# Threshold attention and a SwiGLU block: one weight join moved behind the masks, value passes ahead of transposes, two more nested groups, and a changed plan for the last part

## The chip, the cores and the metric

The kernel runs on one core of a Trainium2 chip. The metric is the time of one execution on the device in microseconds (us); lower is better. Engines are named as the profile names them: PE is TensorE (matrix products and transposes), DVE is VectorE, ACT is ScalarE, POOL is GpSimd, SP is the engine that issues the DMAs.

## The reference

```python
# q, k, v: (8 batches, 8 heads, 576, 64) fp32; tau = 0.02
scores = matmul(q, k^T) / sqrt(64)
thresh = max(scores, -1) - tau
scores = where(scores >= thresh, scores, -1e9)
scores = scores - max(scores, -1)
attn = exp(scores); attn = attn / (sum(attn, -1) + 1e-9)
x = matmul(attn, v)            # -> (4608 tokens, 512)
g = x @ w_gate                 # w_gate, w_val: (512, 1536)
out = (g * sigmoid(g) * (x @ w_val)) @ w_out   # w_out: (1536, 512)
```

Everything is fp32, results included.

## The kernel before

The heads are taken in pairs, 32 in all, four for each batch. The kernel has three parts.

**The first part (0 to about 129 us)** works through batch 0 in eight passes, `n` = 0 to 7, in an order written out by hand: passes 0 to 3 take the first two query tiles of each of the four pairs, passes 4 to 7 the remaining three, of which the last is a short tile (`t == NT`). For each tile TensorE computes scores into a PSUM bank (L484), VectorE takes the maximum (L501), ScalarE the exponential (L505), and VectorE the mask, which multiplies by "score at or above the threshold" and sums (L508). The masks are the last readers of the scores' banks, one for each head. Then the rows are scaled by the reciprocal of the sum (ScalarE L518, POOL L516), transposed on TensorE (`tp`, L552 and L554, the rest in `end`, L560), copied out by ScalarE (L561), and multiplied with the values (`attend`, L585 and L587). A generator for each tile, `go`, is advanced step by step, and the loop places other work between its steps:

- `fill(part)` issues products of the feed-forward block's first weights for tokens that are there already (`pg`, `pv`, L601), as many as `pace` gives to a tile. ScalarE reads `pg` at L616 and L617.
- The weights of the block come from HBM in pieces. A piece is fetched by two DMAs on SP (`fetch_weights`, L332), split by ScalarE into an upper and a lower word (`split_weights`, L348 and L349), clamped by POOL (L341), shifted by VectorE (L368), joined by VectorE with the sign bits (`join_weights`, L374), and its lower part is added by POOL (`add_lower`, L384). `join_weights` takes all the pieces that were shifted, which is two after a short tile: that tile calls `shift_weights(2)`. It stands right behind the maxima, ahead of the tile's exponentials and masks.

**The middle (129 to about 1127 us)** takes batches 1 to 7 in 28 passes of three tiles each, 84 slots. The order on TensorE is written out; that of VectorE, ScalarE, POOL and SP comes from a planner. `Plan` keeps a list of open jobs for each of these engines. A job has a length in us (`took`), dependencies, a rank (a lower one goes first among those that are ready within .2 us) and a delay of its result (`lag`). `pe()` puts work on TensorE, advances the plan's clock, and makes the jobs that start before it issue their instructions. The lengths are constants in the code, so the order is fixed when the kernel is built. `slot_rest` holds the jobs of one slot: maxima, exponentials (L2104), masks (L2106), the exchange of sums (`xj`, ScalarE L2115), sum and reciprocal (`rj`, VectorE L2120 and L2121), scaling (ScalarE L2133, POOL L2130), transposes on VectorE (L2135). `POOLED` says how many of a slot's scalings are POOL's.

The tokens of the feed-forward block go in nine chunks `c` of 512: chunks 0 to 7 are the first 512 rows of each batch, chunk 8 the last 64 rows of all eight. Between the slots' products the gate and value products of a chunk that is complete are placed, in six groups `g` by `gates_and_values(c)`. A `Group` computes a 2x2 block product with seven products instead of eight: blocks of weights and of tokens are added before, and results after. One product is four matmuls of 128x128 by 128x256 (L1138). In a `NestedGroup` the products p5 and p3 are split once more, each into seven matmuls of 128x128 by 128x128 (L1333); their inputs are made by `deepen_x` on VectorE, the results are copied by ScalarE (L1271, L1273) and added up by `fold`, four additions on VectorE or POOL (helpers at L929 and L926). `deep = c > DEEP and g in WITH_BLOCKS`, with `DEEP = 2` and `WITH_BLOCKS = (1, 2, 3)`, chooses between them. The class `Deep` does the output product in the same manner, with inner sums of gated values (`inner_sums`), results combined from two PSUM banks (`combine`, L2018 and L2020 on VectorE), and deepened products `px`, `py` (L1768).

**The last part (from about 1127 us)** has no attention tile left. `tail[0]` is set, the tokens of the last two chunks, 7 and 8, are deepened (`deepen_all`), twelve groups of class `Whole` follow, six for each chunk (products L2543; L2593 is ScalarE's tanh of a folded gate, L2595 multiplies it with the value on VectorE, L2615 and L2625 add a product to a sum and are the last readers of its PSUM bank), and then the output products of `Deep(7)` and `Deep(8)`, whose sums end in `out_dram`.

Of the kernel before, what the change touches and what calls it, by code (L numbers as in the profile page):

```python
# [14 lines left out]
ALU = mybir.AluOpType  # L15
# [12 lines left out]
class Plan:  # L28
# [3 lines left out]
    HOP, PIPE = 0.08, 0.22  # L32
    PATIENCE = 0.2
    AGE = 12.0

    def __init__(self):
        self.t = self.moved = 0.0
        self.free = dict.fromkeys(("DVE", "ACT", "POOL", "SP"), 0.0)
        self.open = {e: [] for e in self.free}

    def job(self, eng, took, fn, *deps, rank=1, lag=0.0, moves=0.0):
# [30 lines left out]
    def step(self):  # L72
        start, e, n = self.peek()
        j = self.open[e].pop(n)
        start = max(start, j.ready)
        j.fn()
        self.free[e] = start + j.took
        j.end = start + j.took + j.lag
        if j.moves:
            self.moved = max(self.moved, start) + j.moves  # L80
            j.end = max(start + j.took, self.moved) + j.lag
# [63 lines left out]
def kernel(  # L145
# [11 lines left out]
    nc = tc.nc  # L157
    P = 128
    B, H, S, D = q.shape
    NP = H // 2  # L160
# [209 lines left out]

    def join_weights():
        for up, place, lo in shifted:
            ub = up.bitcast(U32)
            nc.vector.scalar_tensor_tensor(out=ub, in0=words(place, up, 1), scalar=0x80000000, in1=ub,  # L374
                                           op0=ALU.bitwise_and, op1=ALU.bitwise_xor)
            used.discard(place)
        unsummed.extend(shifted)
        shifted.clear()
        add_lower(min(1, len(unsummed)))
# [407 lines left out]
    for n, seg in enumerate(segs[:2 * NP]):  # L787
        early_slots[0] = n < NP
        if n >= NP:
            seg["v"] = segs[seg["i"]]["v"]  # L790
        for x, t in enumerate(seg["tiles"]):
            assert n < NP or seg["i"] in turned_rests
            go = scores(seg, t)
            next(go)
            steps(n, x, "maxima")
            if n >= NP:
                join_weights()
            if not n and not x:
                run_idle(6)
            next(last, None)  # L800
            box = []
            if n < NP:
                attend_tile(lambda *y: box.extend(y))
            else:
                attend_tile()
            flips = flip_steps()
            if n >= NP and x == 1:
                next(flips, None)
            next(go)
            if box:  # L810
                box[1]()
                give_back(box[0])
            next(last, None)
            for _ in flips:
                pass
            if n == NP and x == 0:
                attend_tile()
                give(FIRST)
            part = pace(n, x) / 2
            more = len(split)  # L820
            if n >= NP:
                split_weights()
                fetch_weights(2)
            steps(n, x, "flipped")
            next(go)
            steps(n, x, "masked")
            double = t == NT and NP <= n < NP + 3
            if n >= NP:
                clamp_split()
                add_lower(1)  # L830
                if more and not double:
                    shift_weights()
            fill(part)
            next(go)
# [90 lines left out]
    def pool_tt(out, a, b, op):  # L925
        return lambda: nc.gpsimd.tensor_tensor(out=out, in0=a, in1=b, op=op)  # L926

    def dve_tt(out, a, b, op):
        return lambda: nc.vector.tensor_tensor(out=out, in0=a, in1=b, op=op)  # L929

# [330 lines left out]
    class Seven(Buf):  # L1261
# [13 lines left out]
        def fold(self, eng, rank, *deps):  # L1275

            y = self.place.rearrange("p (x q) -> p x q", q=P)
            tt, took, less = (dve_tt, 0.36, 0.23) if eng == "DVE" else (pool_tt, 0.85, 0.52) if tail[0] else (pool_tt, 0.75, 0.44)
            twice = lambda x: y[:, x:x + 1].broadcast_to((P, 2, P))
            j = job(eng, took, tt(y[:, 1:3], twice(0), y[:, 1:3], ALU.add), *deps, rank=rank)  # L1280
            j = job(eng, took, tt(y[:, 0:7:6], twice(2), y[:, 5:7], ALU.add), j, rank=rank)
            j = job(eng, less, tt(y[:, 2], y[:, 0], y[:, 3], ALU.add), j, rank=rank)
            return job(eng, took, tt(y[:, 4:6], twice(6), y[:, 4:6], ALU.add), j, rank=rank)

# [390 lines left out]
    class Deep:  # L1675
# [65 lines left out]
        def inner_sums(self, o, a, place, ready, *deps):  # L1741

            a11, a21, a12, a22 = quarters(a)
            flat = place if len(place.shape) == 2 else place.rearrange("p f n -> p (f n)")
            s1, s2, s3, s4 = (flat[:, n * QW:(n + 1) * QW].rearrange("p (f q) -> p f q", q=P) for n in range(4))
            tt, eng, took = (dve_tt, "DVE", 0.55) if tail[0] else (pool_tt, "POOL", 1.0)
            rank = 0 if o == 1 and self.c == B - 1 else 0 if o == 1 else 1 if o == 5 or o in (3, 6) and not tail[0] or o in (0, 6) and tail[0] or self.c == B - 2 else 2
# [45 lines left out]
        def combine(self, q, *deps, psum=False):  # L1793
# [13 lines left out]
            else:  # L1807
                tt, eng, took, less, rank = (dve_tt, "DVE", 0.36, 0.23, 1) if tail[0] else (pool_tt, "POOL", 0.75, 0.44, 2)
            twice = lambda x: x.broadcast_to((P, 2, P))
# [147 lines left out]
        def p5(self):  # L1957
# [3 lines left out]
            state["free_cells"] = lambda *deps, m=m: self.free_cells((5, 6), m, *deps)  # L1961
            n, j = self.combine(t7, job("POOL", 2.2, pool_tt(t7, t7, t, ALU.add), *self.c5, *self.c7, rank=1))
            self.ship(1, 1, n, j)
# [99 lines left out]
    def slot_rest(seg, t, pss, mark, pooled, max_by_act, rank):  # L2063
# [52 lines left out]

        xj = job("ACT", 0.78, exchange, *masks.values(), rank=1)

# [3 lines left out]

        rj = job("DVE", 0.36, total, xj, rank=1)
        sum_users[-1].append(rj)
# [101 lines left out]
    def gates_and_values(c):  # L2226
# [5 lines left out]
        for g in range(NF2):  # L2232
            deep = c > DEEP and g in WITH_BLOCKS
            new = NestedGroup(c, g) if deep else Group(c, g)
# [42 lines left out]
    CH = {0: 2, 1: 3, 10: 4, 11: 4}  # L2277
    POOLED = {0: 3, 1: 1, 2: 1, 3: 3, 4: 3, 5: 2, 6: 1, 7: 2, 8: 1}
    MAX_BY_ACT = (0, 1, 3, 4, 5, 6, 8, 9)
# [13 lines left out]
    def block_part(b, kk):  # L2293
# [17 lines left out]
        if kk in GV:  # L2311
            if kk == 1:
                state["gv"], state["c"] = gates_and_values(c), c
                if c > DEEP:
                    deepen_x(c, *(j for js in streamed_kept.values() for j in js))
# [22 lines left out]
    for s, (n, x) in enumerate((n, x) for n in range(len(halved)) for x in range(NU3)):  # L2338
# [21 lines left out]
        if s == 1:  # L2360
            prepare_v(seg)
        at_, pooled, max_by_act = (kk, POOLED, MAX_BY_ACT) if b > DEEP else (s, FIRST_POOLED, FIRST_MAX_BY_ACT)
        slot_rest(seg, t, pss, mark, pooled.get(at_, 0), at_ in max_by_act, 1 if x == NU3 - 1 else 2)
# [27 lines left out]

    tail[0] = True
    last_x = []
# [15 lines left out]
    load_last(1, 1, attended)  # L2409
    state["free_cells"](attended)  # L2410

# [20 lines left out]
    def deepen_all(c, eng, rank, lo, n, step, fourth, *deps, last=()):  # L2432
# [5 lines left out]
        t4 = deep_places[c][2][:, os_] if fourth is None else fourth  # L2438
        tt, took = (dve_tt, 0.15 + 0.18 * n) if eng == "DVE" else (pool_tt, 0.2 + 0.32 * n)
        j = job(eng, took, tt(t1, b12, b11, ALU.subtract), *deps, rank=rank)  # L2440
# [272 lines left out]
```

## Time and profile before

| what | value |
|---|---|
| time, median of 3 runs | 1345.34 us (1344.86 to 1345.55) |
| the profiled execution: its own time | 1344.29 us |
| the profiled execution: its span | 1342.4 us |
| mean granted TensorE clock | 0.999 |
| PE busy | 1327.0 us, 99% of the span |
| DVE, ACT, POOL busy | 1082.9, 899.1, 932.8 us (81%, 67%, 69%) |
| DMA moved | 209.81 MB, 156 GB/s in the mean |

All start times in this text are us from the start of the span. The profile records each fp32 matmul twice, so counts of matmul rows are twice the program's. "Busy" is time in which an engine executes; instructions that issue a DMA or wait are not counted. A row of a timeline gives the start, the length, the engine, the line, the operation, what it writes and reads, the shape, and a count where equal instructions follow each other; in square brackets stands the idle time ahead of it and what ended it. The name of a buffer in a row is that of its place in memory, which many values share in turn.

### The profile page before, as it was taken

The page shows a single profiled execution, that of the slowest core. Times are in us where ns is not written, and L with a number is a line of the kernel's source. Part 1 is how long each engine was busy: PE and PEld are TensorE (multiplying, and loading weights), DVE is VectorE, ACT ScalarE, POOL GpSimd, SP SyncE. Part 2 cuts the span into 40 slices and gives each one's busy share as a digit, 9 for nine tenths or more (in the row PEclk, how much of TensorE's full clock was granted, in tenths as well). Part 3 has the DMA queues.
Part 4 walks back from the last instruction along what each step waited for, and adds up shares of the span by engine and source line. Part 5 has one row for each costly group of instructions (what it writes and reads, how often), then busy time and mean ns, then how long its engine had stood idle before and what let it go on. Part 6 is the DMA issues. An engine that isn't in the chain of part 4 may idle for free. (4 is left out here: it accounts for less than half of the span.)

```text
span 1342.4 us, 41686 instructions
## 1 busy us (share of the span) xinstructions
PE 1327.0 (99%) x16274; PEld 1123.1 (84%) x16274; DVE 1082.9 (81%) x2891; ACT 899.1 (67%) x2341; POOL 932.8 (69%) x1115
## 2 busy tenths in 40 slices
PE   9999999999999999999999999999999999999998
PEld 7777877787887878888888888888888889999998
DVE  7888898888887778888888887888888887667886
ACT  6888777767756677787777777777777775344300
POOL 2688497565685759857895779677976799856720
PEclk9999999999999999999999999999999999999999
DMA  8852424356557553656365746655474627565241
GB/s 180 205 188 92 85 58 134 122 150 178 154 166 220 174 167 89 208 165 219 76 201 168 232 111 187 178 168 149 115 214 146 213 68 232 158 202 183 88 169 40
DMA packets 230884, 209.81 MB, mean 156 GB/s; under 512 B 167968, under 2 KB 185376, under 8 KB 223008
## 3 DMA queue, kind: packets, MB, share of 16 engines
q1 hardware_dynamic: 226768, 206.22, 52.2%
q8 instruction: 129, 2.11, 0.7%
q10 hardware_dynamic: 3920, 0.92, 0.3%
q14 instruction: 67, 0.55, 0.1%
HBM read 169.08 MB, written 38.01 MB: 154 GB/s over the span
## 5 line engine op out<-in xcount | busy, mean ns | idle before, releaser
L2106 DVE SCALAR_TENSOR_TENSOR pall<-sc,th,pall 128x288 f32<-128x288 f32 x504 | 244.2, 513 | 42.6 <-ACT pall L2104 23.4
L2104 ACT ACTIVATE pall<-sc,nm 128x288 f32<-128x288 f32 x504 | 232.9, 498 | 35.3 <-DVE pall L2106 34.9
L2135 DVE STREAM_TRANSPOSE pall<-pall 128x576 f32<-128x576 f32 x252 | 188.3, 764 | 22.1 <-ACT pall L2133 12.1
L1138 PE MATMUL pb<-xall,big 128*128 128x256 f32 x864 | 205.8, 381 | 0.0
L2133 ACT ACTIVATE pall<-pall,ri 128x288 f32<-128x288 f32 x388 | 178.9, 527 | 27.7 <-DVE ri L2121 26.9
L926 POOL TENSOR_TENSOR big<-big 128x128 f32<-128x128 f32 (+3 forms) x214 | 158.9, 751 | 46.5 <-ACT big L1273 20.8
L1138 PEld LDWEIGHTS pb<-xall,big 128*128 128x128 f32 x864 | 161.2, 190 | 24.0 <-issue 2.2
L926 POOL TENSOR_TENSOR hall<-hall,tmp 128x512 f32<-128x512 f32 x80 | 102.3, 1279 | 95.6 <-DVE hall L1197 75.9
L2079 DVE TENSOR_REDUCE mx<-sc 128x2 f32<-128x576 f32 x168 | 125.7, 748 | 39.7 <-PE sc L2058 39.3
L2058 PE MATMUL sc<-kT,qT 64*32 64x288 f32 (+1 forms) x5376 | 145.3, 345 | 0.4 <-DVE pall L2106 0.4
L1138 PE MATMUL pa<-xall,big 128*128 128x256 f32 x576 | 137.7, 382 | 0.0
L2058 PEld LDWEIGHTS sc<-kT,qT 64*32 64x32 f32 x5376 | 96.2, 106 | 48.6 <-issue 9.3
L2157 PE MATMUL xa<-pall,vall 64*32 64x288 f32 x4032 | 129.4, 404 | 0.5 <-PE px L1768 0.4
L1138 PEld LDWEIGHTS pa<-xall,big 128*128 128x128 f32 x576 | 107.8, 190 | 17.5 <-issue 2.5
L2157 PEld LDWEIGHTS xa<-pall,vall 64*32 64x32 f32 x4032 | 75.6, 107 | 46.6 <-issue 5.0
L2130 POOL TENSOR_SCALAR pall<-pall,ri 128x288 f32<-128x288 f32 x116 | 58.2, 513 | 53.1 <-DVE ri L2121 52.8
L1138 PE MATMUL pe<-xall,big 128*128 128x256 f32 x384 | 91.4, 381 | 0.0
L2115 ACT COPY sums<-sums 32x6 f32<-32x6 f32 x336 | 66.6, 198 | 30.3 <-DVE pall L2106 25.2
L1138 PEld LDWEIGHTS pe<-xall,big 128*128 128x128 f32 x384 | 72.4, 190 | 11.1 <-ACT pall L2133 0.7
L2081 DVE TENSOR_REDUCE mx<-sc 128x1 f32<-128x288 f32 x168 | 75.0, 447 | 0.0
L926 POOL TENSOR_TENSOR hall<-hall 128x384 f32<-128x384 f32 (+2 forms) x69 | 70.0, 1028 | 0.8
L1196 ACT ACTIVATE vall<-tmp 128x512 f32<-128x512 f32 x72 | 45.1, 627 | 35.6 <-POOL tmp L926 19.0
(365 smaller groups left out, 3051.6 us busy)
## 6 DMA issues: line engine op xcount, KB each, us to landing
big<-sums_hbm SPq DMA_DIRECT2D x30, 1280.0 KB, 7.9
big<-sums_hbm SPq DMA_DIRECT2D x30, 1024.0 KB, 7.8
vall<-in_v_dram SPq DMA_DIRECT2D x112, 144.0 KB, 3.5
big<-sums_hbm SPq DMA_DIRECT2D x54, 256.0 KB, 3.6
sums_hbm<-big SPq DMA_DIRECT2D x36, 256.0 KB, 3.8
out_dram<-big SPq DMA_DIRECT2D x32, 256.0 KB, 2.8
qT<-in_q_dram SPq DMA_DIRECT2D x112, 72.0 KB, 4.0
kT<-in_k_dram SPq DMA_DIRECT2D x112, 72.0 KB, 3.0
```

Source lines behind the costliest of these rows:

```text
L926: return lambda: nc.gpsimd.tensor_tensor(out=out, in0=a, in1=b, op=op)
L1138: nc.tensor.matmul(ps[:, i], w[:, k_, i * P:(i + 1) * P], x[:, k_, :], start=first and i == k_ == 0, stop=True, skip_group_check=True)
L2058: nc.tensor.matmul(pss[h][(slice(g * G, (g + 1) * G), *part)], qT[hs, col:col + G], kT[hs, c * SH + keys[0]:c * SH + keys[1]], start=True, ...
L2079: rs.append(job("DVE", 0.72, lambda n=n, tile_=tile_: nc.vector.tensor_reduce(out=mx[:, n:n + 2, 0], in_=tile_[:, :, 0:SH], axis=AX.X, op= ...
L2081: rs.append(job("DVE", 0.42, lambda n=n, tile_=tile_: nc.vector.tensor_reduce(out=mx[:, n + 2:n + 3, 0], in_=tile_[:, :, SH:SH + SQ], axis ...
L2104: ej = job("ACT", 0.42, lambda x=x, n=n: nc.scalar.activation(ps[x], scs[x], AF.Exp, bias=nm[:, n:n + 1]), ej, masks.get((h, u - 1)), rank=0)
L2106: masks[x] = job("DVE", 0.45, lambda x=x, n=n: nc.vector.scalar_tensor_tensor(out=ps[x], in0=scs[x], scalar=th[:, n:n + 1], in1=ps[x], op0 ...
L2115: nc.scalar.copy(sm[g * G:(g + 1) * G, 0:m, 1], sm[o * G:(o + 1) * G, 0:m, 0])
L2130: scaled.append(job("POOL", 0.48 if seg["i"] >= 3 * NP else 0.4, lambda x=x, n=n: nc.gpsimd.tensor_scalar(out=x, in0=x, scalar1=ri[:, n:n ...
L2133: scaled.append(job("ACT", 0.46, lambda x=x, n=n: nc.scalar.activation(x, x, AF.Copy, scale=ri[:, n:n + 1]), rj, rank=rank))
L2135: seg["turned"].append(job("DVE", 0.72, lambda both=both: nc.vector.transpose(out=both, in_=both), *scaled, rank=rank))
L2157: nc.tensor.matmul(holds[a].ap()[x * G:(x + 1) * G, 0:SH].rearrange("d (i q) -> d i q", q=G), vr[rs, h, j, ds], p[rs, h, :, j, :], start=( ...
```

## The change

It has three pieces.

1. In the first part, `join_weights` gets a count. Behind the maxima one piece is joined; what is left is joined behind the masks, and the two fetches that its place allows are issued there. In the short tile of passes 4 to 7 half of the tile's `fill` is issued ahead of the transposes, and the other half is halved again for the two places behind.
2. Groups 2 and 3 of chunk `c = 2` become nested: `deep` is `c >= DEEP` with `WITH_BLOCKS[1:]` at `c == DEEP`, and `deepen_x` is called for that chunk too.
3. For the last part the planner gets new numbers: a model in which VectorE and POOL lengthen each other where jobs with all operands in SBUF overlap (`SLOWED`, used once `plan.shares` is set together with `tail[0]`), other lengths for folds, inner sums and deepening, a delay of .3 for folds, other ranks for the inner sums, the deepening of chunk 8 and the last tile's sums, POOL for two scalings of the last tile, a later due time of the freed cells, and VectorE instead of POOL for one addition and one combination of `Deep(7)`.

```diff
@@ Plan
+    SLOWED = {"DVE": 0.45, "POOL": 0.2}
...
-        self.free[e] = start + j.took
-        j.end = start + j.took + j.lag
+        took = j.took
+        if self.shares and e in self.SLOWED and getattr(j.fn, "in_sbuf", False):
+            for x, (k, end) in self.last.items():
+                if x != e and end > start:
+                    both = min(end - start, took)
+                    took += both * self.SLOWED[e]
+                    k.end += both * self.SLOWED[x]
+                    self.free[x] = max(self.free[x], k.end - k.lag)
+                    for i in k.then:
+                        i.ready = max(i.ready, self.after(k, i.eng))
+            self.last[e] = j, start + took
+        self.free[e] = start + took
+        j.end = start + took + j.lag
@@ first part
-    def join_weights():
-        for up, place, lo in shifted:
+    def join_weights(n=None):
+        steps = shifted[:n]
+        for up, place, lo in steps:
...
-        unsummed.extend(shifted)
-        shifted.clear()
+        unsummed.extend(steps)
+        del shifted[:n]
         add_lower(min(1, len(unsummed)))
...
             if n >= NP:
-                join_weights()
+                join_weights(1)
...
+            first_fill = n >= NP and t == NT
+            if first_fill:
+                part = pace(n, x) / 2
+                fill(part)
             next(go)
...
-            part = pace(n, x) / 2
+            part = part / 2 if first_fill else pace(n, x) / 2
...
             if n >= NP:
+                if shifted:
+                    join_weights()
+                    fetch_weights(2)
                 clamp_split()
@@ NestedGroup.fold
-... else (pool_tt, 0.85, 0.52) if tail[0] else (pool_tt, 0.75, 0.44)
+... else (pool_tt, 0.73, 0.46) if tail[0] else (pool_tt, 0.75, 0.44)
...
-            return job(eng, took, tt(y[:, 4:6], twice(6), y[:, 4:6], ALU.add), j, rank=rank)
+            return job(eng, took, tt(y[:, 4:6], twice(6), y[:, 4:6], ALU.add), j, rank=rank, lag=0.3 if tail[0] else 0.0)
@@ Deep.inner_sums
-            tt, eng, took = (dve_tt, "DVE", 0.55) if tail[0] else (pool_tt, "POOL", 1.0)
-            rank = 0 if o == 1 and self.c == B - 1 else 0 if o == 1 else 1 if o == 5 or ...
+            tt, eng, took = (dve_tt, "DVE", 0.48) if tail[0] else (pool_tt, "POOL", 1.0)
+            rank = 0 if o == 6 and self.c == B else 0 if o == 1 and self.c == B - 1 else 1 if o == 1 and tail[0] else 0 if o == 1 else 1 if o == 5 or ...
@@ Deep.combine
-                tt, eng, took, less, rank = (dve_tt, "DVE", 0.36, 0.23, 1) if tail[0] else (pool_tt, "POOL", 0.75, 0.44, 2)
+                tt, eng, took, less, rank = (dve_tt, "DVE", 0.36, 0.23, 1) if tail[0] or self.c == B - 2 and self.blocks > 1 else (pool_tt, "POOL", 0.75, 0.44, 2)
@@ Deep, p5
-            n, j = self.combine(t7, job("POOL", 2.2, pool_tt(t7, t7, t, ALU.add), *self.c5, *self.c7, rank=1))
+            tt, eng, took = (dve_tt, "DVE", 1.05) if self.c == B - 2 else (pool_tt, "POOL", 2.2)
+            n, j = self.combine(t7, job(eng, took, tt(t7, t7, t, ALU.add), *self.c5, *self.c7, rank=1))
@@ slot_rest
-        xj = job("ACT", 0.78, exchange, *masks.values(), rank=1)
+        first = -1 if seg is halved[-1] and t == seg["tiles"][-1] else 1
+        xj = job("ACT", 0.78, exchange, *masks.values(), rank=first)
...
-        rj = job("DVE", 0.36, total, xj, rank=1)
+        rj = job("DVE", 0.36, total, xj, rank=first)
@@ gates_and_values
-            deep = c > DEEP and g in WITH_BLOCKS
+            deep = c >= DEEP and g in WITH_BLOCKS[c == DEEP:]
@@ slots
-    POOLED = {0: 3, 1: 1, 2: 1, 3: 3, 4: 3, 5: 2, 6: 1, 7: 2, 8: 1}
+    POOLED = {NS: 2, 0: 3, 1: 1, 2: 1, 3: 3, 4: 3, 5: 2, 6: 1, 7: 2, 8: 1}
...
-                if c > DEEP:
+                if c >= DEEP:
                     deepen_x(c, ...)
@@ last part
-    tail[0] = True
+    tail[0] = plan.shares = True
...
-    state["free_cells"](attended)
+    state["free_cells"](attended, plan.t + 2.5)
...
-        tt, took = (dve_tt, 0.15 + 0.18 * n) if eng == "DVE" else (pool_tt, 0.2 + 0.32 * n)
+        tt, took = (dve_tt, 0.08 + 0.14 * n) if eng == "DVE" else (pool_tt, 0.18 + 0.275 * n)
...
-    deepen_all(B, "DVE", 0, 0, 1, 1, None, j3, *free)
+    deepen_all(B, "DVE", -1, 0, 1, 1, None, j3, *free)
...
-    deepen_all(B, "DVE", 0, 2, 2, 2, None, j4, x_ready[B, 0])
+    deepen_all(B, "DVE", -1, 2, 2, 2, None, j4, x_ready[B, 0])
```

More of the change, by code (lines that the diff above doesn't have):

```diff
@@ L39, in __init__ @@
         self.open = {e: [] for e in self.free}
+        self.shares, self.last = False, {}
     def job(self, eng, took, fn, *deps, rank=1, lag=0.0, moves=0.0):
@@ L76, in step @@
         j.fn()
-        self.free[e] = start + j.took
-        j.end = start + j.took + j.lag
+        took = j.took
[11 more added lines that the diff above has]
+        j.end = start + took + j.lag
         if j.moves:
             self.moved = max(self.moved, start) + j.moves
-            j.end = max(start + j.took, self.moved) + j.lag
+            j.end = max(start + took, self.moved) + j.lag
         for k in j.then:
@@ L925, in pool_tt, with fn @@
     def pool_tt(out, a, b, op):
-        return lambda: nc.gpsimd.tensor_tensor(out=out, in0=a, in1=b, op=op)
+        def fn():
+            nc.gpsimd.tensor_tensor(out=out, in0=a, in1=b, op=op)
+        fn.in_sbuf = True
+        return fn
     def dve_tt(out, a, b, op):
-        return lambda: nc.vector.tensor_tensor(out=out, in0=a, in1=b, op=op)
+        def fn():
+            nc.vector.tensor_tensor(out=out, in0=a, in1=b, op=op)
+        fn.in_sbuf = not any(x.space == bass.MemoryType.PSUM for x in (a, b))
+        return fn
     def rest_of_weights():
@@ L1277, in fold @@
             y = self.place.rearrange("p (x q) -> p x q", q=P)
-            tt, took, less = (dve_tt, 0.36, 0.23) if eng == "DVE" else (pool_tt, 0.85, 0.52) if tail[0] else (pool_tt, 0.75, 0.44)
+            tt, took, less = (dve_tt, 0.36, 0.23) if eng == "DVE" else (pool_tt, 0.73, 0.46) if tail[0] else (pool_tt, 0.75, 0.44)
             twice = lambda x: y[:, x:x + 1].broadcast_to((P, 2, P))
@@ L1745, in inner_sums @@
             s1, s2, s3, s4 = (flat[:, n * QW:(n + 1) * QW].rearrange("p (f q) -> p f q", q=P) for n in range(4))
-            tt, eng, took = (dve_tt, "DVE", 0.55) if tail[0] else (pool_tt, "POOL", 1.0)
-            rank = 0 if o == 1 and self.c == B - 1 else 0 if o == 1 else 1 if o == 5 or o in (3, 6) and not tail[0] or o in (0, 6) and tail[0] or self.c == B - 2 else 2
+            tt, eng, took = (dve_tt, "DVE", 0.48) if tail[0] else (pool_tt, "POOL", 1.0)
+            rank = 0 if o == 6 and self.c == B else 0 if o == 1 and self.c == B - 1 else 1 if o == 1 and tail[0] else 0 if o == 1 else 1 if o == 5 or o in (3, 6) and not tail[0] or o in (0, 6) and tail[0] or self.c == B - 2 else 2
             j3 = job(eng, took, tt(s3, a11, a21, ALU.subtract), *ready, *deps, rank=rank)
@@ L2361 @@
             prepare_v(seg)
-        at_, pooled, max_by_act = (kk, POOLED, MAX_BY_ACT) if b > DEEP else (s, FIRST_POOLED, FIRST_MAX_BY_ACT)
+        at_, pooled, max_by_act = (kk if n + 1 < len(halved) or x + 1 < NU3 else NS, POOLED, MAX_BY_ACT) if b > DEEP else (s, FIRST_POOLED, FIRST_MAX_BY_ACT)
         slot_rest(seg, t, pss, mark, pooled.get(at_, 0), at_ in max_by_act, 1 if x == NU3 - 1 else 2)
```

## The prediction

> **What bounds the kernel now.** I read the page's busy totals first, then TensorE's waits, then the timelines around each wait, TensorE's first and then that of the engine which ended it.
>
> ```profile
> PE 1327.0 (99%) x16274; PEld 1123.1 (84%) x16274; DVE 1082.9 (81%) x2891; ACT 899.1 (67%) x2341; POOL 932.8 (69%) x1115
> ```
>
> TensorE is busy for 1327.0 of 1342.4 us, so only 15.4 us of idle time can be taken away, besides work of its own. The table of its waits (waiting operation, releaser: total us, times, longest) says where most of it lies.
>
> ```profile
> PE sc L484 <- DVE pall L508: 3.0, 5, 1.1
> ...
> PE sc L2543 <- DVE tmp L2625: 0.9, 1, 0.9
> PE px L1768 <- DVE big L929: 0.9, 1, 0.9
> ...
> PE sc L2543 <- ACT tmp L1273: 0.5, 1, 0.5
> PE xa L2157 <- PE px L1768: 0.4, 1, 0.4
> ...
> PE tp L552 <- POOL qT L424: 0.4, 1, 0.4
> PE tp L552 <- POOL big L341: 0.4, 1, 0.4
> ```
>
> The lines below 600 belong to the first part, the others to the last 220 us. The windows from 400 to 900 us hold no idle time of TensorE at all: there only its own work counts.
>
> **First part, the joins.** VectorE's timeline in the sixth of the eight passes (start, length, operation):
>
> ```profile
> 73.07 2.76 DVE L374 SCALAR_TENSOR_TENSOR big<-wo,big 128x768 uint32<-128x768 uint32 x2
> 75.75 0.81 DVE L508 SCALAR_TENSOR_TENSOR pall<-sc,th,pall 128x576 f32<-128x576 f32 x1
> ```
>
> and TensorE's:
>
> ```profile
> 76.71 1.03 PE L484 MATMUL sc<-pall 64*128 64x288 f32 x4 [0.80 <-DVE pall L508]
> ```
>
> Two joins stand ahead of the first mask, and the scores of the next tile wait for the mask to free their bank. The change joins one there and the other behind both masks. One join beside POOL is about 1.4 of the 2.76, so the masks could start at 74.5; the exponentials, ready at about 74.2, allow it. The bank that was freed at 76.6 is then freed at about 75.3, ahead of 75.91, where TensorE ran dry. The .80 goes. In the seventh pass (two joins 3.00, wait .62 at 96.38) it goes too. In the eighth, at 116.04, the wait is 1.05, and behind one join alone the exponential comes last: I count .95. Sum .80 + .62 + .95 = 2.37.
>
> The second join moves into VectorE's next gap: 1.25 us idle at 80.5 to 81.7, and 1.66 in the tile after. Without that cover its 1.0 to 1.4 us would stand ahead of a maximum, L501, and the wait would come back one tile later. The move also shifts one pair of weight DMAs on SP behind eight query and key loads, from 53.1 to about 60.3. It would land at 65 to 66, and its split on ScalarE is at 68.6: some 2 us of cover. On POOL the lower addition (L384) now runs ahead of the clamp (L341); nothing on TensorE waits for either before the next tile.
>
> **First part, value passes.** In the short tile of passes five to eight, 3, 3, 2 and 2 value matmuls (L601, .43 each, so 1.29 or .86 us) now run ahead of the transposes instead of behind. The waits they cover:
>
> ```profile
> 86.64 0.63 PE L552 MATMUL tp<-pall 128*128 128x128 f32 x4 [0.35 <-POOL big L341]
> ```
>
> with .16 before it, so .51 in pass six; .13 + .36 in pass five, .15 + .36 in pass seven, .32 in pass eight, together 1.83. The profile names POOL, but L617 on ScalarE, reading the gate's bank, ends .1 before each: the covering work need only be longer than .5, and is. The .32 of pass eight is given back at 139.07, where scores wait for a mask whose chain hangs on a DMA and not on TensorE: 1.51 stays. The price could be a later L561 on ScalarE (.3 to .4), which has that much slack before TensorE's next use in these passes. First part together: 2.37 + 1.51 = 3.9; from 2.5 (half of the joins' share returns as ScalarE's wait) to 4.2.
>
> **Middle, two more nested groups.** At c = 2 the groups 2 and 3 become nested: four products of four 128x256 matmuls become seven 128x128 each. Such a pair of rows stands at 582 us: eight records (four matmuls, two passes each) from 582.65 to 584.38, 1.73 us, and fourteen from 584.38 to 585.94, 1.56 us. So 4 x .17 = .7 us of TensorE is saved, all of it on the path. POOL gets three folds of four operations, 3 x (3 x .75 + .44) = 8.1 us by the code's lengths. POOL idles for 9.9 + 8.8 us of the windows 460 to 500, but only 2.3 us of 500 to 560. If half the folds spilled there, the banks would come free up to 4 us late, and a bank asked for at 468.1 is now free at 466.9, with 1.2 us in hand. So the bounds are a gain of .7 and a loss of 4.0 - 1.2 - .7 = 2.1; I take .7, as most of the folds fall due before 490, in the stretch with idle time. The four deepening additions that VectorE gets (at most 1 us each) and ScalarE's two further copies lie in windows where these engines have 4 to 8 us idle of 20.
>
> **The last 220 us.** Here the planner's lengths, ranks and a model of DVE and POOL delaying each other are changed; TensorE's order stays, the other queues' changes. Five places:
>
> 1126.85, idle .42: the last tile's transposes were late because two VectorE operations waiting for a product (1121.78 to 1122.85) stood ahead of the sum and reciprocal, and six scalings took ScalarE 2.67. Now the sum goes first, at 1121.45, and POOL does two scalings: 1.3 + .9 us earlier, so the .42 goes.
>
> 1166.77, idle .53: ScalarE's L2593 waited for a POOL fold (1161.57 to 1165.19). The fold's first operation now goes into a POOL gap of .63 ahead of a 1.28 product, so the fold ends about .6 earlier: .5 gone.
>
> 1272.84, idle .94:
>
> ```profile
> 1270.15 1.57 DVE L929 TENSOR_TENSOR big<-hall,big 128x384 f32<-128x384 f32 x1
> 1271.65 1.14 DVE L2625 SCALAR_TENSOR_TENSOR tmp<-sc,tmp 128x512 f32<-128x512 f32 x2
> ```
>
> The two are swapped; L2625 then ends at about 1271.3, ahead of 1271.9 where TensorE ran dry: .94 gone. The sums behind it come about 1 us later and are needed 1.9 us after their new end.
>
> 1313.41, idle .91:
>
> ```profile
> 1310.40 2.28 DVE L929 TENSOR_TENSOR xall<-xall 128x384 f32<-128x384 f32 x4
> 1312.60 0.28 DVE L929 TENSOR_TENSOR big<-big,pall 128x128 f32<-128x128 f32 x1
> 1312.80 0.55 DVE L929 TENSOR_TENSOR big<-big 128x384 f32<-128x384 f32 x1
> ```
>
> TensorE waited for the last row, which the change puts first, at about 1308: .91 gone. The four displaced operations, 2.28 us, end at about 1316.3 and feed a product at 1317.1, .7 us in hand.
>
> 1121 to 1130: a 128x896 addition moves from POOL (2.10) to VectorE (about 1.05) with its combination. VectorE idles 2.9 us at 1126.7 to 1129.6, which covers it; with that gone it would push back L929 at 1129.65 by 1 us, and TensorE was without any idle time until 1133.
>
> VectorE's 128x384 addition with both inputs in SBUF takes .55 alone (1312.80) and 1.57 where a POOL operation ran from 1270.04 to 1271.31: it was blocked till then and took .55 after. The new plan counts such a meeting as a share, .55 x 1.45 = .80, so its due times can be .8 early. [...]
>
> **Sum.** 3.9 + .7 + .4 + .5 + .9 + .9 = 7.3 us. I take .4 off for small new waits, such as the .7 us in hand: 6.9. The profiled run took 1344.29 (span 1342.4 and 1.9 around it), 1.05 below the median of 1345.34. So 1337.4 on the profiled run's scale, 1338.4 on the median's.
>
> **Rivals.** A: the tail's four waits (2.7 us) reappear beside their old places. For: each swap leaves displaced work close behind, and VectorE is busy for 28.57 of 30 us in 1260 to 1290. Against: the margins above, .6 to 1.9. Then 1338.4 + 2.7 = 1341.1.
>
> B: the first part's 3.9 comes back, because ScalarE and VectorE run near their limit there and the moved join finds no gap. For: the gap is 1.25 and a join up to 1.4. Then 1338.4 + 3.9 = 1342.3.
>
> C: the folds at c = 2 hold a bank. With 2.8 us of new waits it is 1338.4 + 2.8 = 1341.2. Two of A, B and C together leave little of the change: A and B 1338.4 + 2.7 + 3.9 = 1345.0, no difference.
>
> D, slower: the plan now counts every POOL fold of the last part .3 later and VectorE's own additions shorter (.48 for .55), so in each of the twelve last groups VectorE's queue can hold another addition (.55 alone, 1.57 beside POOL) ahead of L2615 or L2625, which free the bank that the next product needs. Beyond 6.9 / 12 = .58 us per group the kernel is slower; at 1.0, the difference of the two lengths, it is 12.0 - 6.9 = 5.1 slower: 1350.4. Against: TensorE has no idle time from 1170 to 1260, and in the first 60 us of these VectorE is busy for 35.2.
>
> That the change does nothing (planner picks the same order) is excluded for the places above, whose order in the queues differs in the changed program.
>
> **Chances.** A measurement of this kernel can tell about 0.2%, 2.7 us: below 1342.65 is faster. Forecast .50, A .19, B .10, C .05, two of them together .07, D .09. The first four are faster, .84 less .03 for B's closeness to the bound: .81. Same .07 + .03 = .10, slower .09. The range leaves out D and the combined case, .16. Its low end is the sum with nothing taken off and the first part at 4.2 (7.6 us, 1337.7), its high end B's 1342.3, each with .7 to .9 more for the spread of the three runs (.69) and of the profiled one: 1336.8 to 1343.0.
>
> **What would show it.** Right: no wait of L484 on L508 above .2 in passes five to eight; L552 without idle time; fewer 128x256 rows around 452 to 477; no waits at the four tail places; TensorE busy 1326.3 of a span of 1335.5. Wrong: a new wait of L484 or L501 near 80 to 82 (B), of pa, pb or pe at 460 to 500 (C), like waits of L2543 in group after group from 1140 (D), or new waits of L1768 at 1316 (A).

## The result, and the profile after

| | before | after |
|---|---|---|
| median (six runs each) | 1345.1 us (1343.39 to 1345.58) | 1339.08 us (1338.94 to 1340.89) |
| ratio, 95% interval | | 0.9964 [0.9954, 0.9974] |
| span of the profiled execution | 1342.4 us | 1338.8 us |
| TensorE busy | 1327.0 us | 1324.7 us |

The change makes the kernel faster: 6.0 us between the medians, 4.8 us (3.5 to 6.2) by the ratio. The forecast was 1338.4. The page's busy totals after:

```profile
PE 1324.7 (99%) x16298; PEld 1122.5 (84%) x16298; DVE 1095.3 (82%) x2904; ACT 900.5 (67%) x2345; POOL 940.2 (70%) x1124
```

VectorE has 12 and POOL 7 us more work, TensorE 24 rows more and 2.3 us less busy time.

TensorE's waits after the change (waiting operation, releaser: total us, times, longest):

```profile
PE sc L498 <- DVE cap L734: 2.0, 1, 2.0
PE sc L498 <- DVE pall L522: 1.9, 3, 0.9
...
PE sc L2088 <- DVE pall L2136: 1.1, 1, 1.1
PE px L1797 <- issue: 1.0, 1, 1.0
PE tp L566 <- ACT pall L532: 0.8, 2, 0.4
PE sc L2574 <- ACT tmp L1302: 0.7, 1, 0.7
...
PE pb L2574 <- ACT tmp L1302: 0.2, 1, 0.2
```

Gone are the waits on L2625, on the inner sum and of the last attend (.94, .91, .42), and those of the transposes on the gate's bank. Still there is one mask wait of .8 (the .9 stands at 18 us, in code that is the same). New are 1.0 in L1797 without a releaser, .7 for ScalarE's L1302, .4 twice in front of transposes, and 1.1 in place of .38 at the first halved tile.

The transposes of the sixth pass now run in one piece, and VectorE's L2656 (L2625 before) stands ahead of the 128x384 addition:

```profile
87.22 1.04 PE L566 MATMUL tp<-pall 128*128 128x128 f32 x8
```
```profile
1268.53 1.14 DVE L2656 SCALAR_TENSOR_TENSOR tmp<-pb,tmp 128x512 f32<-128x512 f32 x2
1269.60 0.55 DVE L955 TENSOR_TENSOR big<-hall,big 128x384 f32<-128x384 f32 x1
```

The addition takes .55 here in place of 1.57.

**A ledger.** TensorE's instructions have the same order in both programs, but for the value passes and the nested products. So the start of each can be compared with the start of the same instruction before. This shows more than lists of idle time: 128x128 matmuls overlap their neighbours by .16 us (those at 1131.69 in the changed kernel are .39 long, and the next start .23 behind), and a stop loses that overlap too. The four pairs of transposes had 1.83 of idle time in the list, and 3.2 us went when they ran without a stop.

| place | forecast | after |
|---|---|---|
| passes five to eight and the first halved tile (54 to 141) | -3.9 | -2.69 |
| chunk 2 (450 to 477) | -.7 | -.65 |
| 1127 | -.4 | -.46 |
| 1131, first output products behind the attend | 0 | +1.07 |
| 1166 | -.5 | -.33 |
| 1253, one of the twelve last groups | 0 | +.94 |
| 1272 | -.9 | -1.20 |
| 1313 | -.9 | -1.17 |
| sum | -7.3 (6.9 after .4 taken off) | -4.5 |

From 54 us to the end TensorE gains 5.0; the rest is -.1 at 1247, and .4 and -.8 at 407 and 1061, two places where the packed 64x32 matmuls of one of the two executions took longer, with no edit near: 64 rows at 407 took 1.70 before and 2.12 after, and 144 rows at 1055 start over 4.99 us before and 4.19 after. The first row has such a share too: e3 and e4 below, whose first part is that of the kernel before, stand .47 and .43 ahead of its trace at 141, where all of them wait for a DMA (see f1) that took 5.44 us in that trace and 4.83 and 4.96 in theirs. Seven traces with the first part of the changed kernel stand between -2.53 and -2.76. The spans differ by only 3.6, because this execution of the changed kernel was already 1.37 late at 54 us. Why is told under the experiments on the clock.

### The profile page after: what moved, and what is told of

Its sections match the earlier page's. It is cut to its first block, busy times and chain, and to the rows that moved or that the text cites. A ratio compares the mean times of both kernels' runs of the same rounds, so it can differ in the third digit from the quotient of the medians.

```text
span 1338.8 us, 41744 instructions
## 1 busy us (share of the span) xinstructions
PE 1324.7 (99%) x16298; PEld 1122.5 (84%) x16298; DVE 1095.3 (82%) x2904; ACT 900.5 (67%) x2345; POOL 940.2 (70%) x1124
## 3 DMA queue, kind: packets, MB, share of 16 engines
q8 instruction: 129, 2.11, 0.6%
## 5 line engine op out<-in xcount | busy, mean ns | idle before, releaser
L948 POOL TENSOR_TENSOR big<-big 128x128 f32<-128x128 f32 (+3 forms) x226 | 168.0, 752 | 50.9 <-ACT big L1302 22.1
L1167 PE MATMUL pe<-xall,big 128*128 128x256 f32 x352 | 83.9, 381 | 0.0
L1167 PEld LDWEIGHTS pe<-xall,big 128*128 128x128 f32 x352 | 66.4, 190 | 10.2 <-ACT xlast L2200 0.7
L948 POOL TENSOR_TENSOR big<-hall 128x384 f32<-128x384 f32 (+2 forms) x69 | 65.6, 974 | 4.3 <-PE pa L1167 4.2
```

What stands on the lines that cost most here:

```text
L1167: nc.tensor.matmul(ps[:, i], w[:, k_, i * P:(i + 1) * P], x[:, k_, :], start=first and i == k_ == 0, stop=True, skip_group_check=True)
```

## Experiments

All ratios are to the kernel before on the same chip. "Ledger" is TensorE's lead or lag as above, from 54 us on, where no edit has yet had effect.

### The four pieces alone

```diff
 e1: before +
+            if first_fill:
+                part = pace(n, x) / 2
+                fill(part)
 e2: before +
-                join_weights()
+                join_weights(1)
...
+                if shifted:
+                    join_weights()
+                    fetch_weights(2)
 e3: before +
-            deep = c > DEEP and g in WITH_BLOCKS
+            deep = c >= DEEP and g in WITH_BLOCKS[c == DEEP:]
 e4: before + everything else (plan, lengths, ranks, engines of the last part)
```

> The kernel before with the value passes ahead of the short tile's transposes, and nothing else of the change. By the prediction's terms the four passes give 1.8 us and .3 is given back at the first halved tile: 1.5 us by 140 us. Rival: a stop of TensorE costs some .2 us more than the idle time that the profile lists, because matmuls overlap their neighbours by about .16 us and a stop takes the overlap away at each side; then the four transposes give 2.8 to 3.0 us, less what is given back at the first halved tile (.4 to .7): 2.3 us or more.

> The kernel before with only the second join moved behind both masks. By the prediction's terms the waits of the scores for the masks fall from .80, .62 and 1.05 to 0, 0 and .10: 2.4 us. Rival: the first join alone is held up for as long as POOL's gating product, started just before it, runs (2.0 us in place of 1.0), so the .80 of the sixth pass stays; in the seventh and eighth the join goes first, the waits of .62 and 1.05 go, but transposes behind wait about .4 each for ScalarE, which waits for POOL's lower addition: .4 to .9 us in all.

> The kernel before with groups 2 and 3 of chunk 2 nested, and nothing else. By the prediction .7 us of TensorE's own work goes between 450 and 477 us, with no new wait of pa, pb or pe behind it. Rival: the folds on POOL are paid for behind 500 us, where it has 2 of 60 us idle; then waits of up to 2.8 us appear there.

> The kernel before with only the changed plan, ranks, lengths and engines of the last part. By the prediction's terms 2.7 us less, with no wait over .2 left at the four places. Rival: the four old waits go (3.0 us with the overlap that each stop loses), but two new ones come, 1.0 us in the output products behind the last attend, where TensorE waits for no semaphore, and .7 us in one of the twelve last groups, where ScalarE's copies stand behind a tanh that waits for a POOL fold: 1.3 us less in all.

| | ratio | ledger |
|---|---|---|
| e1 value passes | 1.0027 [1.0018, 1.0036] | +2.6 by 141: slower |
| e2 joins | 0.9978 [0.9968, 0.9987] | -2.5 by 141 |
| e3 nested | 1.0005 [0.9996, 1.0014] | -.65 at 475, +.55 at 1131 |
| e4 last part | 0.9989 [0.9979, 0.9998] | -2.1 from 1100 on |

*e1* refutes both expectations. The transposes' stops are gone, but the next tile's scores wait the longer for the masks: 1.71, 1.38 and 1.91 in place of .80, .62 and 1.05, 2.5 us in all. Its sixth pass, TensorE:

```profile
78.13 2.59 PE L484 MATMUL sc<-pall 64*128 64x288 f32 x10 [1.71 <-DVE pall L508]
```

The scores start at 78.13, as they would have without the edit (76.71, and 1.41 for this execution's late start). So most of what the transposes win, the mask takes back. The slowdown comes from the clock, which was halved behind this stop (below) and cost 3.2 us: without that the ledger would stand at about -.6. The mean granted clock is .994 to .997 in all ten runs of e1, and .997 to 1.000 in those of the kernel before.

*e2* confirms the forecast's 2.37 for the joins alone, and not the rival: the ledger stands at -2.6 by 128, ahead of the wait for the DMA. The waits of L484 on L508 go in all three passes, though the first join of the sixth pass took 1.93 beside POOL here too: TensorE, still stopped at its transposes, comes later.

*e3*: TensorE's own .65 is saved, and .55 is lost again where no one forecast it, at the first output products of the last part. The time does not change.

*e4* loses the four old waits but for one, and has new ones: .80 at 1165 (it was .53) and .54 at 1254, both for ScalarE's copies. The rival's 1.0 behind the last attend did not come.

### The changed kernel with one piece taken away or moved

```diff
 f1: after, short tile
-                part = pace(n, x) / 2
-                fill(part)
 f2: after, deep = c > DEEP and g in WITH_BLOCKS again
 f3: after, gating product of the double tile one place later
                 join_weights(1)
+                gates()
...
-            gates()
+            if not double:
+                gates()
 f4: after, start
-    run_idle(6)
+    run_idle(10)
```

> The changed kernel without its value passes ahead of the short tile's transposes; all else of the change stays. If the value passes add their 1.5 to 3 us to the other pieces, this is 1341 to 1342 and the waits of the transposes are back with nothing else. Rival: the value passes and the join spend the same slack, since the next tile's masks hang on VectorE and ScalarE and not on TensorE; then by 141 us TensorE stands within .4 us of the changed kernel, and the time is the same.

> The changed kernel with the groups 2 and 3 of chunk 2 plain as before. If the wait of 1.0 us at the first output products behind the last attend is late code, whose block boundary the twelve added matmuls moved to that place, the wait is gone: .65 us more at 475 us, 1.1 to 1.2 less at 1131, so the same time or .5 us less. Rival: the wait comes from the additions that VectorE has now at that place, or from the output stores that they release 5 us earlier; then it stays, and the kernel is .65 us slower.

> The changed kernel with the gating product that POOL does behind the double tile queued one place later, behind the lower addition of the first join. If it is this product that holds up the join in the sixth pass (started .06 us ahead of it, 2.03 us in place of 1.0), the join takes 1.0 there, the wait of .82 at 77.2 is gone, and in the two passes behind it the lower addition starts some 1.1 us earlier, so the waits of .40 and .39 of the transposes go too: 1.2 to 2 us less by 130 us, of which the halved tile at 138 may take back up to 1. Rival: the masks hang on the exponentials, and nothing changes by more than .2.

> The changed kernel with ten idle products at the start in place of six. In the changed kernel's profile they end at 5.83, TensorE stands still for 2.05 us, and the granted clock is halved from 8.1 to 11.5; in the profile of before they end at 6.68, it stands still for 1.17, and no half clock follows. If the stop halves the clock, four more products keep it full in every run: the slower ones of the runs, 1.3 to 1.9 us above the others, are gone, and the median falls by up to .5 us. Rival: the clock's windows run free of the kernel, and the half clock comes as before; then the spread stays. All code of TensorE moves by four instructions, so the wait at 1131 may change too.

*f1*, ratio 0.9969 [0.9957, 0.9981]: as the rival says, with a link in the chain that it does not name, a DMA. The transposes' stops are back and TensorE is up to 1.0 us later in between, but the scores of the first halved tile start at 137.73 here and at 137.75 in the changed kernel, because the wait there is .05 in place of 1.10. The masks it waits for start at 136.05 here and at 136.08 in the changed kernel. VectorE stands idle ahead of them. In the changed kernel (VectorE's last join of the first part, the fetch of weights that it lets go, the split of these weights on ScalarE, the mask):

```profile
128.56 0.98 DVE L388 SCALAR_TENSOR_TENSOR wo<-xall,wo 128x768 uint32<-128x768 uint32 x1
129.61 0.37 SPq L342 DMA_DIRECT2D xall<-in_moe_w_out_dram  x1
134.73 0.93 ACT L982 ACTIVATE wo<-xall 128x768 f32<-128x768 f32 x1 [1.14 <-DMA xall<-in_moe_w_out_dram]
136.08 0.52 DVE L2136 SCALAR_TENSOR_TENSOR pall<-sc,th,pall 128x288 f32<-128x288 f32 x1 [1.26 <-ACT pall L2134]
```

The exponentials stand behind the split on ScalarE, and the split waits for the DMA. In f1 the join ends .28 later and the DMA is issued at 129.89, but it takes 4.80 us in place of 5.10, so that the split starts at 134.71. That the two meet within .02 is luck; that they meet within .3 is not. Once the joins are out of the way, this chain sets the end of the first part, and the value passes only move the place where TensorE waits.

*f2*, ratio 0.996 [0.9947, 0.9973], median 1338.71: the wait at 1131 is gone, as expected of late code, and from 54 us on TensorE gains .5 on the changed kernel. The additions on VectorE and the early output stores are still in it, so they are not the cause. Where the stop falls says more. TensorE behind the attend, in the changed kernel and in f4, whose four more products at the start are four more matmuls ahead of this place:

```profile
1128.51 1.27 PE L1797 MATMUL px<-wo,hall 128*128 128x128 f32 x9
1130.81 0.60 PE L1797 MATMUL px<-wo,hall 128*128 128x128 f32 x3 [1.03 <-issue]
```
```profile
1126.92 0.38 PE L1797 MATMUL px<-wo,hall 128*128 128x128 f32 x1
1128.46 1.49 PE L1797 MATMUL px<-wo,hall 128*128 128x128 f32 x11 [1.17 <-issue]
```

The stop comes behind nine rows in the one and behind one row in the other: eight rows earlier, which are four matmuls of two rows each. The stop hangs on the place in the program, not on data. In the changed kernel, e3, f1, f3, g1 and g4, all with nesting and the same count of matmuls, it stands at the same row (1.03, .37, 1.27, 1.13, .28, 1.72); in the kernels without nesting there is none. TensorE's code came by a 16 KB transfer that began at 1128.42 (the DMA share was 1.06 from 1126 to 1128), and TensorE went on 2.39 us behind that. In all seven traces with the stop it goes on 2.3 to 2.7 us behind the start of such a transfer, so the stop is long where the transfer starts late against TensorE's arrival. In f2, which has no stop, TensorE comes to the same count of rows 3.14 us behind it. The changed kernel's page has 129 such transfers, 2.11 MB, on one of its two instruction queues, q8, for 32596 rows of matmuls and weight loads, 253 for each; that they bring TensorE's code is read from this and from the times. The shift by exactly four matmuls agrees with a border between two transfers at this place, and twelve added matmuls moved it there. That the queue's load made the code late was not tried by itself.

*f3*, ratio 0.9973 [0.9963, 0.9984]: the cause of the remaining mask wait is right, the gain is not. In the changed kernel POOL's product and VectorE's join of the sixth pass:

```profile
74.23 1.27 POOL L646 TENSOR_TENSOR hall<-hall,tmp 128x512 f32<-128x512 f32 x1
```
```profile
74.29 2.03 DVE L388 SCALAR_TENSOR_TENSOR big<-wo,big 128x768 uint32<-128x768 uint32 x1
```

POOL starts .06 us earlier, and the join ends .82 after it: it was held for the whole product. In f3 the join takes .94 and the wait of .82 is gone:

```profile
72.89 0.94 DVE L388 SCALAR_TENSOR_TENSOR big<-wo,big 128x768 uint32<-128x768 uint32 x1
```

But POOL's product now stands ahead of its scaling L530, which takes 1.72 beside the second join, and transposes (.42) and scores (.41) wait for that. By 141 the ledger is .9 worse than the changed kernel's. The wait went round the three engines and came back.

*f4*, ratio 0.9965 [0.9952, 0.9977]: this execution has no half clock at the start, and the mean granted clock is 1.000 in all five runs, where the two slowest of the changed kernel's six in the result have .999. But the five runs spread from 1338.72 to 1340.6, so the half clock at the start is not all of the spread; what the rest is stays open. The late code's stop, .28 to 1.72 from trace to trace, would be wide enough for it.

### The plan of the last part

```diff
 g1: after, (pool_tt, 0.73, 0.46) -> (pool_tt, 0.9, 0.75) in fold
 g2: after without nesting, (pool_tt, 0.85, 0.52) in fold
 g3: after without nesting, (pool_tt, 0.9, 0.75) in fold
 g4: after
-    tail[0] = plan.shares = True
+    tail[0] = True
```

> The changed kernel with the planner's length for a POOL fold of the last part set to what its rows show (four additions in 3.4 to 3.6 us: .9 each and .75 for the shorter one, in place of .73 and .46). If the .68 of idle time at 1253 comes from ScalarE's order, a tanh queued ahead of two copies because the plan has the fold end .6 us too early, the copies go first there and the wait is gone, as is the one of .21 to .5 at 1165: .7 to 1.1 us less. Rival: the order changes elsewhere too and other groups wait as much; no gain.

> The changed kernel without the two nested groups, and with the planner's fold lengths of before (.85 and .52), the delay of .3 kept. Without nesting the late code at 1131 is away (f2: .5 us less than the changed kernel in all); if .85 is long enough for ScalarE's order, the waits at 1163 and 1251 (.86 and .53 in f2) go as well: 1.2 to 1.6 us less than f2, about 1337.3. Rival: the waits stay; 1338.7.

> As the kernel before this one, with fold lengths of .9 and .75. Same expectation: 1337.3 if the fold's length sets ScalarE's order at both places, 1338.7 if it does not.

> The changed kernel without the planner's model of VectorE and POOL lengthening each other; lengths, ranks and engines as changed. If the model is what takes L2656 out from behind a 128x384 addition and so the wait of .94 at 1272, that wait is back, .9 to 1.1 us more. Rival: the ranks and lengths do it, and the time is the same within .3 us.

The wait at 1253 in the changed kernel, ScalarE's queue first and then TensorE:

```profile
1251.61 0.63 ACT L2624 ACTIVATE kT<-xall 128x512 f32<-128x512 f32 x1 [1.96 <-POOL xall L948]
1252.15 0.47 ACT L1300 ACTIVATE tmp<-sc 128x384 f32<-128x384 f32 x1
1252.52 0.59 ACT L1302 ACTIVATE tmp<-sc 128x512 f32<-128x512 f32 x1
```
```profile
1253.16 0.71 PE L2574 MATMUL sc<-xall,big 128*128 128x128 f32 x4 [0.68 <-ACT tmp L1302]
```

L2624 is the tanh of a gate that POOL folds; the two copies that TensorE needs stand behind it. The fold takes 3.53 us, and the plan counts 2.65 for it.

*g1* (0.996 [0.9947, 0.9972]), *g2* (0.9963 [0.9951, 0.9976]) and *g3* (0.9957 [0.9945, 0.9970]): in all three the waits at 1165 and 1253 are gone, as expected of a fold that the plan takes for too short. But ScalarE's order changed elsewhere too, and a new wait of 1.2 stands 4 us behind the first place in each, in g1:

```profile
1166.44 0.68 PE L2574 MATMUL pe<-pall,big 128*128 128x128 f32 x4 [1.22 <-ACT sc L2588]
```

g2 has one of .49 at 1275 besides. So the cause is right, and for the sum the rival: behind 1131 g1 wins 1.4 us on the changed kernel at the two places, loses as much at the new one, and ends as the changed kernel does. g2 comes to 1339.24 and g3 to 1338.19, where 1337.3 was expected. g3 has the lowest median of all, but its interval overlaps that of the changed kernel; which of the two is faster is not settled.

*g4*, ratio 1.0013 [1.0004, 1.0022], median 1346.14: slower than the kernel before and some 7 us slower than the changed kernel, where 1.1 was expected. The wait at 1272 does not come back, so the ranks and lengths are enough to move L2656; but another wait comes:

```profile
1284.78 7.50 PE L1806 MATMUL py<-wo,hall 128*128 128x256 f32 x22 [4.44 <-DVE big L955]
```

VectorE's combination, which frees the bank, starts at 1283.45 behind three 128x512 sums that take 2.95 us from 1280.57. The likely reason, which was not tried, is that with the shorter lengths and without the model the plan believes VectorE to be done earlier than it is. The other new numbers of the last part do need the model: without it they are slower than the old plan.

### The clock

Two of these stops cost more than their length. The granted clock in windows of 3.4 us, as long as the half clock at the changed kernel's start (8.11 to 11.52), of e1 and of g4 (window: us, busy us of TensorE and of its weight loads, of VectorE, ScalarE, POOL, then clock, DMA share, GB/s):

```profile
76.10:79.50 3.40, 1.69 (x10) 1.29 (x9) 3.33 (x10) 1.95 (x5) 2.67 (x2) 1.00 0.57 153
79.50:82.90 3.40, 3.40 (x26) 2.51 (x25) 2.87 (x4) 1.34 (x3) 3.29 (x3) 0.50 0.78 312
82.90:86.30 3.40, 3.40 (x13) 2.95 (x12) 2.29 (x4) 2.96 (x8) 1.82 (x1) 0.50 0.47 123
```
```profile
1279.60:1283.00 3.40, 0.73 (x7) 0.54 (x5) 3.40 (x5) 0.97 (x2) 1.58 (x1) 1.00 0.00 1
1283.00:1286.40 3.40, 1.62 (x4) 1.39 (x5) 3.26 (x8) 0.00 (x0) 0.00 (x0) 0.51 0.32 115
```

Behind the first window of each, in which TensorE was busy for 1.69 and .73 us, it ran at half speed for 6.8 us, and the ledgers lose 3.2 and 2.6 us there besides the stop (in g4 TensorE stood still for the first 1.75 of the 6.8). The start shows the same. In the changed kernel's profile TensorE stood still for 2.05 of the window from 4.7 to 8.1, and the clock was .5 to 11.5; in the profile of before for 1.17, with no half clock. In all traces with 1.95 us or more of it (after, e1, e2, f1) the half clock follows and TensorE is 1.4 to 1.6 us late at 54 us; in those with 1.80 or less it does not. The stop is long where the full clock comes early, since the idle products then end early (at 5.83 in the changed kernel, at 6.68 in that of before): the clock's record turns to full between 4.4 and 4.9 us in these four, and between 5.2 and 7.0 in the other nine with six idle products. f4, with ten, tells the two apart: full clock from 4.22, a stop of .83, and no half clock. So it is the stop, as far as one trace can show it. The length alone is not a full rule: 1.71 was enough at 78.13 in e1, but 1.91 at 120.5 in e1, also within one window, left the clock at 1.00.

## Why the prediction was right or wrong

**Right: the sign, the range, and what bounds the kernel.** All of the gain was taken out of the listed idle time and the .65 of TensorE's own work. No wait was left at three of the four places of the last part. That the median came within .7 us of the forecast is partly luck. The ledger gains 5.0 where 6.9 was forecast, and the 1.05 that the prediction added to get from its profiled run to the median of three made up for half of the difference.

**Wrong: the first part's sum, 3.9 for 2.7.** Each term was about right by itself or too small: joins 2.37 (e2: 2.5), transposes 1.83 (3.2 by the ledger). What failed was the adding up. The prediction saw that at 139.07 the scores wait for a mask "whose chain hangs on a DMA and not on TensorE", and gave back the eighth pass's .32 there. But that chain takes back whatever TensorE alone has won, from all four passes: the changed kernel stands at -3.4 by 128, f1 at -2.4, and they at -2.7 and -2.8 by 141. Value passes beside the joins are worth nothing (f1). Alone they win .6, which the halved clock turns into a loss of 2.6 (e1). This is the forecast's rival B in part, but not by the cause it names: the moved join found its gap, and a fetch of weights behind VectorE's last join sets the end. Two new waits of the transposes also cost .74 and .60 in the ledger, in the seventh and eighth pass: ScalarE's scaling stands behind a split of weights that waits .56 for POOL's lower addition, and that addition is late because POOL's product took 1.98 beside the join.

**Wrong: the price of a join beside POOL.** Half of 2.76 for one of two was the wrong reading: the first is held for as long as POOL's product lasts (2.03), the second takes .96. Which engine starts first, by .06 us in the sixth pass and by .20 the other way in the seventh, decides it. The prediction had read the like off a row under the last part, 1.57 beside POOL for .55 alone, and did not use it here. Its reading there, .55 behind POOL's end, was .41 (1271.72 less 1271.31).

**Wrong: chunk 2, .7 for nothing.** The .65 came as worked out, with no wait of a bank (rival C did not happen), but with twelve more matmuls TensorE stopped at the first output products behind the last attend, by f2 and f4 for code that came late: +1.07. No wait in the trace of before gives a price for that; the prediction's bound, a loss of 2.1, covered it by size and not by cause.

**Half right: the last part.** 2.7 was forecast, 2.3 is there without the late code. Three waits went as said, by 2.8 us. The fold's wait at 1166 went down by .33 only, and a new one that cost .94 came at 1253 by what the prediction gave as rival D, an order that trusts a shorter fold; it came in one group of the twelve, not in all, and on ScalarE's queue, not on VectorE's.

The .4 taken off for small new waits stood for 2.0 us of them in the last part (1.07 and .94).

**The plan's model** counts a meeting of VectorE and POOL as a share. The prediction's doubt of it was right for the meetings: the addition at 1270 of the kernel before took 1.57, where the share makes .80 of its .55, and the held join 2.03 in place of .94. But with these lengths a model by shares is still some 7 us better than none (g4).

## What to carry to other kernels

Add up gains along the chain that is next, not place by place: where two edits free TensorE ahead of the same chain of other engines (here a join, a fetch and a split of weights), only the one that also moves the chain is paid. A hand-made plan's lengths belong together: the model of the two engines' meeting alone decides between 1339 and 1346 us here. And compare the starts of the same instructions of two traces; it shows in one column where time was won and given back, under a run-to-run spread of 2. Places without an edit show its noise: mostly under .1 us here, but .4 to .8 at three places.

## What the runs showed of the hardware

- A stop of TensorE of 1.71 us in one window was followed by 6.8 us at half clock, and one of 4.44 too (e1, g4); this cost 3.2 and 2.6 us more than the stop. One of 1.91 us at another place left the clock at 1.00 (e1, 120.5).
- TensorE stopped for .28 (g1) to 1.72 us (g4), with no releaser in the trace, always at a fixed place of the program, which moves with the count of matmuls ahead of it; it went on 2.3 to 2.7 us behind the start of a 16 KB transfer on an instruction queue. So late code is the likely cause.
- A join on VectorE takes .93 to .96 alone. Where it begins .1 us or more ahead of the end of a POOL operation on SBUF that is under way, it ends .81 to .84 behind the end of that one, and takes up to 2.03 (74.29; all in the changed kernel). Where the join begins first (92.95 there), POOL's product of 1.27 takes 1.98.
